# A kernel with a scheduler of its own: block counts, a load's place, a queue, row halves and stream shares are changed

## The chip, the cores and the metric

The kernel runs on one core of a Trainium2 chip. The metric is device time of one launch in microseconds (us), the median of several runs. TensorE is called PE here, VectorE DVE, ScalarE ACT, GpSimd POOL and SyncE SP, as the profile does.

## The reference

The program computes a forward pass and its gradient for all inputs but one. Cut to what matters:

```
xn  = layernorm(A_q)                                  # 2048 tokens x 512
ks  = sum over t<4 of shifted(A_k, 3-t) * shift_k     # a causal filter of 4 taps
kv  = ks * A_v
y   = causal_conv(kv, ssm_k) + kv * ssm_D             # by FFT of length 4096
s   = xn * y
h   = sigmoid(xn @ w_gate) * (xn @ w_up)              # 512 -> 1376
out = A_q + s * silu(h @ w_down)                      # 1376 -> 512
# returned: out, and the gradients for A_q, A_k, A_v, shift_k, ssm_k, ssm_D, w_gate, w_up, w_down
```

All tensors are bf16.

## The kernel before

**Recording and ordering.** The kernel doesn't issue its instructions as Python meets them. A recorder (`Rec`) takes every call with what it reads and writes. `Rec.order` then lists them: it keeps a modelled clock for each engine, takes the operation that can start first (ties by the order of recording), chooses ACT or DVE for copies that either can make (`evac`), and assigns PSUM banks. `emit` issues the program in that order, so one line of the code carries nearly all instructions: L566 those of PE in groups (bursts), L568 all others.

**Blocks in that model.** The model counts PE's instructions, two for each matmul (a weight load and the matmul), in blocks of `IBLK` = 256. `fetch` (L394) lets PE wait where a block ends sooner than a given time after the block before it. That time is 5.0 us for operations recorded before the mark `rec.late`, and one of the two values of `IFETCH` after it, the larger when the modelled hardware DMA queue is occupied. The count starts from `iblk` (L392). Where a short-tile burst would wait, a dense one may be taken ahead of it.

**Streams.** What is recorded when is set by `run_streams`: generators yield the amount of PE work that they have recorded, and the one with the lowest position goes on. The position runs from the first to the second of two shares (the last two numbers of each tuple), in step with the work done. A stream with a later start share, or a larger end share, is recorded later against the others.

**Stages.** In the first stage, `strG` computes layernorm, gate and up (eight pairs of token tiles), `strK` transforms the convolution kernel, and `strV` filters k, transforms kv, multiplies, and transforms back. Then `stepB` does the gate's backward pass. The last stage runs three streams: `dW` (weight gradients, dense matmuls 512, 352 and 320 wide from transposed loads), `frontC` (forward transform of the convolution's incoming gradient), and `backC`, inside `endC` (products with the stored spectra in DRAM, inverse transforms). `backC` handles four channel groups; after groups 1 and 3 it calls `taps` (L1416) for two groups each.

**`taps`** multiplies the convolution's gradient by v into `dks`, whose last three of nineteen rows hold rows of the neighbouring partitions, copied by two DMAs from `dks` itself. There is one `dks` buffer, so one group's taps wait for the last reader of the group before. `taps` then computes the gradient for shift_k on PE (groups of 128x32 matmuls) and the gradient for k as four multiply-and-add steps over sixteen rows of 128 channels, each a DVE operation of 2048 elements, and stores it to `o2C` in two halves after the second group of a pair.

**The start.** `make_identity` and four small memsets stand on POOL ahead of two small loads: `skT` (filter taps) and `Dcol_b` (ssm_D, the skip weights). POOL adds the skip weights to the first column of the convolution kernel (`KT`). DVE then copies `KT` into another order, and PE transposes it.

Of the kernel before, what the change touches and what calls it, by code (L numbers as in the profile page):

```python
# [10 lines left out]
ALU = mybir.AluOpType  # L11
# [6 lines left out]
P = 128  # L18
# [6 lines left out]
NJ = 16  # L25
# [138 lines left out]
class Rec:  # L164
# [3 lines left out]

    NEAR = 300
    BUBBLE = 0.12  # L170
    IBLK, IFETCH = 256, (4.2, 6.0)
    late = 1 << 30
    hold = None
    ENGS = ("tensor", "vector", "scalar", "gpsimd", "sync")
# [183 lines left out]
    def order(self):  # L358
# [30 lines left out]
        pipe = {"gpsimd": 0.0, "hw": 0.0, "act": 0.0}  # L389
        table = "sin"  # L390
        pemode = "full"
        iblk = [0, 0.0, self.IFETCH[0]]  # L392

        def fetch(op, t, occ, commit):  # L394
            n = 2 * (len(op.alts[0][2]) if op.alts[0][1] == "burst" else 1)
            k, b, gap = iblk
            wait = 0.0
            if k + n >= self.IBLK:
                wait = max(0.0, b + gap - (t + occ * (self.IBLK - k) / n))
                b = t + wait + occ * (self.IBLK - k) / n  # L400
                k -= self.IBLK
                gap = 5.0 if op.n < self.late else self.IFETCH[pipe["hw"] > b + 3.0]
            if commit:
                iblk[:] = [k + n, b, gap]
            return wait
# [166 lines left out]
def run_streams(streams, until=None):  # L572

    live = [list(st) + [0.0] * (5 - len(st)) for st in streams]
    while live:
        if until is not None and until():
            break
        for st in sorted(live, key=lambda s: s[2] + (s[3] - s[2]) * s[4] / s[1]):
            try:
                c = next(st[0])  # L580
            except StopIteration:
                live.remove(st)
                break
            if c:
                st[4] += c
                break
        else:
            raise RuntimeError("all streams blocked")
    return live


def make_identity(nc, ident):
    nc.gpsimd.memset(ident, 0.0)
    nc.gpsimd.affine_select(out=ident, in_=ident, compare_op=ALU.not_equal, fill=1.0,
                            base=0, pattern=[[-1, ident.shape[1]]], channel_multiplier=1)
# [64 lines left out]
def kernel_impl(ctx, tc, A_q, A_k, A_v, A_shift_k, A_ssm_k, A_ssm_D, B_x, B_w_gate, B_w_up, B_w_down,  # L660
# [25 lines left out]
    def dma2o(eng, dst, src):  # L686
        for r in range(2):
            eng.dma_start(dst[r], src[64 * r:64 * r + 64])
# [243 lines left out]
    def ld_w(eng, f0, f1):  # L932
        for w, src in ((wg, B_w_gate), (wu, B_w_up)):
            eng.dma_start(w[:, :, f0:f1], src[:, f0:f1].rearrange("(db p) f -> p db f", p=P))
    make_identity(nc, ident)
    nc.gpsimd.memset(kT[:, 0:16], 0.0)
    nc.gpsimd.memset(wg[:, :, F:FP], 0.0)
# [5 lines left out]
    for eng, r in ((nc.sync, 0), (nc.scalar, 1)):  # L943
        eng.dma_start(T[0]["xq"][64 * r:64 * r + 64], qC[r, :, 0:2, :])
    ld_w(nc.scalar, 0, 512)
    nc.gpsimd.dma_start(skT, A_shift_k.rearrange("(cg p) t -> p cg t", p=P))
    nc.gpsimd.dma_start(Dcol_b, A_ssm_D.rearrange("(cg p) -> p cg", p=P))
    ld_KT(0)
    ld_w(nc.sync, 512, 1024)
    ld_w(nc.sync, 1024, F)  # L950
# [34 lines left out]
    def strG():  # L985
        for q in range(8):
            if q == 0:
                n0 = len(rec.ops)
                f_ln(1)
                rec.ops[n0].deps.add(ln0 + 7)  # L990
                f_Tpe(1)
            if q + 2 < 8:
                f_ln(q + 2)
            if q + 3 < 8:
                f_x(q + 3)
            z = z_pre(q - 1) if q - 1 in ZA else iter(())
            for n, c in enumerate(f_gen(q)):
                yield c
                if n in (1, 3):
                    yield from islice(z, 1)  # L1000
            if q + 2 < 8:
                f_T(q + 2)
            if q == 1:
                nc.sync.dma_start(wd[:, 0:NFB - 1, :], B_w_down[0:128 * (NFB - 1), :].rearrange("(fb p) d -> p fb d", p=P))
                nc.sync.dma_start(wd[0:96, NFB - 1, :], B_w_down[128 * (NFB - 1):F, :])
# [104 lines left out]
            if cg % 2 == 1:  # L1110
                yield from inv1(B, y2A[:, :, c0 - GW:c1])

    run_streams([(strG(), 8 * 22528 + len(ZA) * 11264, -0.06, 1.07), (strK(), 4 * 8192, -0.14, 0.73), (strV(), 4 * 27648, -0.06, 0.97)])
    for r in (KT_r, KC_r, zt_r, kTp_r, kT_r, dg4_r, vg_r, acc_r, V_r, U_r, KS_r, XS_r, P1_r, B_r):
        r.free()

# [299 lines left out]
    def taps(cg):  # L1416
        c0, c1 = cg * GW, (cg + 1) * GW
        dkv = y2A[:, :, c0:c1]
        while "v" not in stC:
            yield 0  # L1420
        vg = stC["v"][:, :, c0:c1]
        dks = dks_r.next()
        nc.vector.tensor_tensor(dks[:, 0:NJ, :], dkv, vg, ALU.mult)
        nc.vector.memset(dks[96:P, NJ:NJ + 3, :], 0.0)
        nc.gpsimd.dma_start(dks[0:64, NJ:NJ + 3, :], dks[64:128, 0:3, :])
        nc.gpsimd.dma_start(dks[64:127, NJ:NJ + 3, :], dks[1:64, 0:3, :])
        nc.vector.tensor_tensor(dkv, dkv, stC["ksh"], ALU.mult)
        if cg + 1 < NG:
            ld_ksh(cg + 1)
        if cg % 2 == 1:  # L1430
            for j in range(0, NJ, 8):
                dma2o(nc.sync, o3C[:, :, j:j + 8, c0 - GW:c1], y2A[:, j:j + 8, c0 - GW:c1])
        yield 512
        pa = nc.ps("m1", [4, 32], f32)
        calls = []
        for j in range(NJ):
            for x in range(4):
                s = slice(32 * x, 32 * x + 32)
                calls.append(("matmul", (pa[s], dks[:, j, s], kh[:, j:j + 4, c0 + 32 * x:c0 + 32 * x + 32]), dict(start=(j == 0), stop=(j == NJ - 1))))
        nc.burst("128x32", 64 * 0.0157, calls)  # L1440
        dm = dm_r.next()
        nc.vector.tensor_tensor(dm, pa[:], I32[:, None, :].to_broadcast([P, 4, 32]), ALU.mult)
        nc.vector.tensor_reduce(res[:, cg, :], dm, AX.X, ALU.add)
        yield 2048
        dk = vg
        for lag in range(4):
            src = dks[:, lag:lag + NJ, :]
            skl = skb[:, lag:lag + 1, c0:c1].to_broadcast([P, NJ, GW])
            if lag == 0:
                nc.vector.tensor_tensor(dk, src, skl, ALU.mult)  # L1450
            else:
                term = dKT_r.next().rearrange("p (j c) -> p j c", c=GW)
                nc.vector.tensor_tensor(term, src, skl, ALU.mult)
                nc.vector.tensor_tensor(dk, dk, term, ALU.add)
            yield 512
        if cg % 2 == 1:
            for j in range(0, NJ, 8):
                dma2o(nc.sync, o2C[:, :, j:j + 8, c0 - GW:c1], stC["v"][:, j:j + 8, c0 - GW:c1])

    def endC():  # L1460
        yield from backC()
# [52 lines left out]
        ld_KK(m)  # L1514
    YS_r = Ring(ar, [2, 1024], n=2)
    V_r, U_r = Ring(ar, [64, 32, 2]), Ring(ar, [32, 32, 2], n=2)
    live = run_streams(live + [(dW(), 35 * 8192, 0.99, 1.42), (frontC(), 8 * 4096, 0.98, 1.42)], until=lambda: "B" in flags)
    pair(7)
    for r in [wgT_r, wuT_r, go_r, L0_r, L1_r, dxa_r, dxn_r, u1_r]:
        r.free()  # L1520
# [10 lines left out]
    ld_KK(2)  # L1531
    rec.late = len(rec.ops)
    dw, fr = live
    live = run_streams([(dw[0], dw[1] - dw[4], 0.0, 1.0), (fr[0], fr[1], 0.03, 0.7, fr[4]),
                        (gated(endC(), "back"), 4 * 20480, -0.05, 0.65)], until=lambda: "back" in flags)
    run_streams(live)
    rec.emit()

# [59 lines left out]
```

## Time and profile before

| | |
|---|---|
| median of 3 runs | 505.82 us |
| lowest and highest run | 499.06 and 506.52 us |
| the profiled execution | 505.26 us |
| its span, first to last instruction | 503.5 us |
| mean granted clock of PE | 0.986 |
| busy share of PE, DVE, ACT, POOL | 92%, 79%, 54%, 4% |
| moved by DMA | 112.74 MB, mean 224 GB/s |

The busy time of PE counts overlapping matmuls once, with modelled ends. In a row of the timeline, the start and the length come first, then engine, line, operation, output and input with shapes, and the count; what stands in brackets is the engine's idle time just before the row and what released it. "Issue" means that the engine waited for nothing that the profile shows. The chip has one PE clock for the core; "granted clock" 0.50 in a window means that it ran at half speed there.

### The profile page before, as it was taken

Reading aid. Unit: us, or ns where it says so; the run is one execution under the profiler, and the core shown is the slowest. Engines: PE = TensorE matmul, PEld = TensorE weight load, DVE = VectorE, ACT = ScalarE, POOL = GpSimd, SP = SyncE. Lnnn points to the kernel's source line nnn. Section 1 sums busy time; section 2 is a strip of 40 time slices with the busy share of each in tenths; the row PEclk is TensorE's granted clock in tenths of the full one; section 3 lists DMA queues with packets and bytes.
Section 4 is the critical chain, followed back from the end, with each engine's and each line's share of the span. In section 5 each row is a group of like instructions: output and inputs, shape, how many; then the busy total and the mean of one; then the engine's idle time right before and its main releaser. Section 6 shows DMA issues by size and latency. Waiting matters only on the chain.

```text
span 503.5 us, 13650 instructions
## 1 busy us (share of the span) xinstructions
PE 464.2 (92%) x5862; PEld 304.1 (60%) x5895; DVE 396.4 (79%) x663; ACT 272.7 (54%) x341; POOL 20.9 (4%) x40
## 2 busy tenths in 40 slices
PE   4999999999999989999999999999898879988984
PEld 3776767686758555566556646445455456666652
DVE  8689999668775699879998998569778479984691
ACT  6567788767665674355266247147466554444211
POOL 4000300000000000000000000100000000000000
PEclk9999999999999989999999999999999889999998
DMA  8999999936599899988978869996899895999954
GB/s 257 213 235 289 244 320 239 301 138 195 196 240 253 224 192 221 292 220 274 269 199 244 197 172 230 227 256 212 197 269 222 215 257 138 247 235 193 196 130 110
DMA packets 180980, 112.74 MB, mean 224 GB/s; under 512 B 101621, under 2 KB 166073, under 8 KB 180920
## 3 DMA queue, kind: packets, MB, share of 16 engines
q1 hardware_dynamic: 179432, 110.29, 88.3%
q10 hardware_dynamic: 1136, 1.18, 0.8%
q8 instruction: 46, 0.75, 0.7%
q0 software_dynamic: 352, 0.40, 0.4%
q14 instruction: 14, 0.11, 0.1%
HBM read 39.23 MB, written 47.62 MB: 172 GB/s over the span
## 4 chain that ended last, share of the span: by engine, by line
PE 61%; issue 13%; DMA 3%; DVE 3%; ACT 2%; POOL 0%; ACTq 0%; POOLq 0%
PE psum L566 61%; DMA slab<-slab 3%; DVE slab L568 3%; ACT slab L568 2%; PE psum L568 0%; POOL slab L568 0%; ACTq L568 0%; POOLq L568 0%
## 5 line engine op out<-in xcount | busy, mean ns | idle before, releaser
L566 PE MATMUL psum<-slab 128*128 128x256 bf16 (+10 forms) x5853 | 462.8, 266 | 31.9 <-issue 10.9
L566 PEld LDWEIGHTS <-slab 128*128 128x128 bf16 (+5 forms) x5886 | 303.4, 102 | 190.4 <-issue 51.4
L568 ACT CAST slab<-psum 128x1024 bf16<-128x1024 f32 (+4 forms) x260 | 214.0, 874 | 170.9 <-PE psum L566 146.7
L568 DVE TENSOR_TENSOR slab<-slab 128x1024 bf16<-128x1024 bf16 (+4 forms) x344 | 242.7, 758 | 24.3 <-ACT slab L568 11.6
L568 DVE CAST slab<-psum 128x1024 bf16<-128x1024 f32 (+2 forms) x34 | 39.5, 1170 | 37.4 <-PE psum L566 20.3
L568 ACT ACTIVATE slab<-psum 128x1024 bf16<-128x1024 f32 (+2 forms) x44 | 37.3, 853 | 33.9 <-PE psum L566 32.7
L568 DVE TENSOR_TENSOR slab<-psum,slab 128x1024 bf16<-128x1024 f32 (+2 forms) x28 | 28.2, 1008 | 13.2 <-PE psum L566 10.4
L568 DVE STREAM_TRANSPOSE slab<-slab 128x512 f32<-128x512 f32 x48 | 31.1, 685 | 3.0 <-ACT slab L568 2.8
L568 ACT ACTIVATE slab<-slab 128x512 bf16<-128x512 bf16 (+3 forms) x25 | 21.8, 889 | 16.5 <-DVE slab L568 16.4
L568 DVE SCALAR_TENSOR_TENSOR slab<-slab 128x512 bf16<-128x512 bf16 (+1 forms) x48 | 24.7, 530 | 3.8 <-ACT slab L568 3.4
L568 DVE TENSOR_SCALAR slab<-slab 128x1 f32<-128x1 f32 (+8 forms) x58 | 13.5, 266 | 2.1 <-POOL slab L568 1.6
L568 POOL TENSOR_TENSOR slab<-slab 128x2 f32<-128x2 f32 (+1 forms) x12 | 9.8, 821 | 79.6 <-DVE slab L568 69.9
L568 POOL MEMSET slab<- 128x128 bf16 (+3 forms) x7 | 3.1, 445 | 214.5 <-PE psum L566 177.8
L568 DVE BATCH_NORM_STATS2 slab<-slab 128x6 f32<-128x512 bf16 x16 | 10.4, 679 | 1.3 <-DMA slab<-in_A_q_dram 1.3
L568 POOL DMA_DIRECT2D slab<-slab x8 | 4.3, 535 | 158.1 <-ACT slab L568 85.2
L568 DVE COPY slab<-slab 128x1216 bf16<-128x1216 bf16 (+2 forms) x17 | 7.2, 446 | 4.2 <-ACT slab L568 4.2
L568 DVE SCALAR_TENSOR_TENSOR slab<-psum,slab 128x512 bf16<-128x512 f32 x10 | 6.7, 686 | 4.5 <-PE psum L566 4.5
L568 ACT ACT_TABLE_LOAD x2 | 2.6, 1283 | 2.5 <-issue 2.5
L568 DVE MEMSET slab<- 32x192 uint32 (+3 forms) x8 | 1.3, 165 | 1.9 <-PEq L1582 0.8
L568 DVE BATCH_NORM_AGGREGATE slab<-slab 128x2 f32<-128x6 f32 x16 | 2.4, 170 | 0.0
L568 PE MATMUL psum<-slab 128*4 128x128 bf16 (+1 forms) x9 | 1.8, 326 | 0.0
L568 POOL DMA_DIRECT2D slab<-in_A_shift_k_dram x2 | 1.5, 769 | 3.0 <-DMA sF_d<-slab 3.0
(15 smaller groups left out, 9.6 us busy)
## 6 DMA issues: line engine op xcount, KB each, us to landing
KK_d<-slab SPq DMA_DIRECT2D x16, 512.0 KB, 4.8
slab<-KK_d SPq DMA_DIRECT2D x16, 512.0 KB, 5.5
out_dram<-slab SPq DMA_DIRECT2D x58, 128.0 KB, 2.8
hS_d<-slab SPq DMA_DIRECT2D x8, 704.0 KB, 6.6
dgS_d<-slab SPq DMA_DIRECT2D x8, 704.0 KB, 4.8
duS_d<-slab SPq DMA_DIRECT2D x8, 704.0 KB, 6.0
sF_d<-slab SPq DMA_DIRECT2D x6, 704.0 KB, 5.7
slab<-sF_d SPq DMA_DIRECT2D x6, 704.0 KB, 6.8
```

Source lines behind the costliest of these rows:

```text
L566: getattr(self.nc.tensor, m)(*[place(v) for v in aa], **{x: place(v) for x, v in kk.items()})
L568: getattr(getattr(self.nc, eng), meth)(*[place(v) for v in a], **{x: place(v) for x, v in k.items()})
```

## The change

Five things change. In the model, `iblk` starts at 96 instead of 0 and without a first wait, the wait of 5.0 us before `rec.late` becomes 0, and the larger value of `IFETCH` becomes 6.5. At the start, the loads of `Dcol_b` and `skT` are recorded ahead of the identity and the memsets. In `taps`, the two row copies are issued by ACT instead of POOL. For the last channel group the four steps run over rows 0 to 7 and then rows 8 to 15, each half with its own store. And the shares of all streams but `stepB` and the remaining `dW` are new.

```diff
-    IBLK, IFETCH = 256, (4.2, 6.0)
+    IBLK, IFETCH = 256, (4.2, 6.5)
...
-        iblk = [0, 0.0, self.IFETCH[0]]
+        iblk = [96, 0.0, 0.0]
...
-                gap = 5.0 if op.n < self.late else self.IFETCH[pipe["hw"] > b + 3.0]
+                gap = 0.0 if op.n < self.late else self.IFETCH[pipe["hw"] > b + 3.0]
...
+    nc.gpsimd.dma_start(Dcol_b, A_ssm_D.rearrange("(cg p) -> p cg", p=P))
+    nc.gpsimd.dma_start(skT, A_shift_k.rearrange("(cg p) t -> p cg t", p=P))
     make_identity(nc, ident)
...
-    nc.gpsimd.dma_start(skT, A_shift_k.rearrange("(cg p) t -> p cg t", p=P))
-    nc.gpsimd.dma_start(Dcol_b, A_ssm_D.rearrange("(cg p) -> p cg", p=P))
...
-    run_streams([(strG(), 8 * 22528 + len(ZA) * 11264, -0.06, 1.07), (strK(), 4 * 8192, -0.14, 0.73), (strV(), 4 * 27648, -0.06, 0.97)])
+    run_streams([(strG(), 8 * 22528 + len(ZA) * 11264, -0.04, 1.02), (strK(), 4 * 8192, -0.07, 0.81), (strV(), 4 * 27648, 0.06, 0.94)])
...
-        nc.gpsimd.dma_start(dks[0:64, NJ:NJ + 3, :], dks[64:128, 0:3, :])
-        nc.gpsimd.dma_start(dks[64:127, NJ:NJ + 3, :], dks[1:64, 0:3, :])
+        nc.scalar.dma_start(dks[0:64, NJ:NJ + 3, :], dks[64:128, 0:3, :])
+        nc.scalar.dma_start(dks[64:127, NJ:NJ + 3, :], dks[1:64, 0:3, :])
...
-        for lag in range(4):
-            src = dks[:, lag:lag + NJ, :]
...
+        step = NJ if cg + 1 < NG else NJ // 2
+        for j0 in range(0, NJ, step):
+            js = slice(j0, j0 + step)
+            for lag in range(4):
+                src = dks[:, lag + j0:lag + j0 + step, :]
...
+            if cg % 2 == 1:
+                for j in range(j0, j0 + step, 8):
+                    dma2o(nc.sync, o2C[:, :, j:j + 8, c0 - GW:c1], stC["v"][:, j:j + 8, c0 - GW:c1])
...
-    live = run_streams(live + [(dW(), 35 * 8192, 0.99, 1.42), (frontC(), 8 * 4096, 0.98, 1.42)], until=lambda: "B" in flags)
+    live = run_streams(live + [(dW(), 35 * 8192, 0.89, 1.91), (frontC(), 8 * 4096, 0.87, 1.62)], until=lambda: "B" in flags)
...
-    live = run_streams([(dw[0], dw[1] - dw[4], 0.0, 1.0), (fr[0], fr[1], 0.03, 0.7, fr[4]),
-                        (gated(endC(), "back"), 4 * 20480, -0.05, 0.65)], until=lambda: "back" in flags)
+    live = run_streams([(dw[0], dw[1] - dw[4], 0.0, 1.0), (fr[0], fr[1], -0.21, 0.48, fr[4]),
+                        (gated(endC(), "back"), 4 * 20480, -0.15, 0.67)], until=lambda: "back" in flags)
```

More of the change, by code (lines that the diff above doesn't have):

```diff
@@ L1445, in taps @@
         dk = vg
-        for lag in range(4):
-            src = dks[:, lag:lag + NJ, :]
[L1448 to L1458, printed above, removed]
+        step = NJ if cg + 1 < NG else NJ // 2
[3 more added lines that the diff above has]
+                src = dks[:, lag + j0:lag + j0 + step, :]
+                skl = skb[:, lag:lag + 1, c0:c1].to_broadcast([P, step, GW])
+                if lag == 0:
+                    nc.vector.tensor_tensor(dk[:, js], src, skl, ALU.mult)
+                else:
+                    term = dKT_r.next().rearrange("p (j c) -> p j c", c=GW)
+                    nc.vector.tensor_tensor(term[:, js], src, skl, ALU.mult)
+                    nc.vector.tensor_tensor(dk[:, js], dk[:, js], term[:, js], ALU.add)
+                yield 32 * step
+            if cg % 2 == 1:
+                for j in range(j0, j0 + step, 8):
+                    dma2o(nc.sync, o2C[:, :, j:j + 8, c0 - GW:c1], stC["v"][:, j:j + 8, c0 - GW:c1])
     def endC():
```

## The prediction

> **What bounds the kernel now.** I read the view by windows first, cut where the work changes: the first stage to 180 us, the gate's backward to 335 us, the last stage to 500 us.
>
> ```profile
> 0.00:180.00 180.00, 165.94 (x2567) 122.47 (x2576) 143.43 (x242) 122.93 (x136) 15.29 (x31) 1.00 0.93 238
> ...
> 335.00:500.00 165.00, 146.25 (x2340) 93.96 (x2347) 122.83 (x158) 77.88 (x104) 4.27 (x8) 0.98 0.89 207
> ```
>
> The columns are the window, its length, then busy time and count for PE, weight loads, DVE, ACT and POOL, then granted clock, DMA share and GB/s. PE is the busiest engine in both rows, DVE is next with 80% and 74%. PE is not busy for 14.1 us of the first stage and 18.8 us of the last, so a better order can win at most these, what the clock costs, and what lies behind the last matmul.
>
> Next I looked at the longest waits of PE in the last stage, in the timeline.
>
> ```profile
> 393.59 2.83 PE L566 MATMUL psum<-slab 64*64 64x64 bf16 x31 [2.40 <-issue]
> ...
> 410.92 36.57 PE L566 MATMUL psum<-slab 128*32 128x128 bf16 x512 [2.76 <-issue]
> ```
>
> Both say "issue": no operand was late. They stand where a block of 128 pairs of weight load and matmul ends, counted from pair 92 of the program. Windows laid between two such places show it: each holds about 128 weight loads (second count).
>
> ```profile
> 354.42:360.87 6.45, 5.25 (x139) 2.94 (x134) 3.75 (x5) 3.29 (x4) 0.00 (x0) 1.00 1.14 228
> 372.60:378.18 5.58, 4.33 (x133) 3.26 (x132) 3.30 (x5) 4.30 (x6) 0.00 (x0) 1.00 1.01 305
> ...
> 386.84:393.58 6.74, 4.34 (x128) 3.22 (x128) 4.32 (x8) 1.92 (x3) 0.00 (x0) 0.99 1.06 276
> 403.14:410.93 7.79, 5.03 (x137) 3.74 (x131) 5.40 (x7) 5.67 (x8) 1.10 (x2) 0.98 1.24 228
> 442.59:448.14 5.55, 5.06 (x142) 3.82 (x134) 3.77 (x7) 2.94 (x5) 0.00 (x0) 1.00 1.11 252
> 457.12:459.97 2.85, 2.22 (x132) 2.08 (x132) 0.00 (x0) 0.63 (x1) 0.00 (x0) 1.00 1.33 148
> ```
>
> These six are the blocks of the last stage with the least work; they took 34.96 us together. PE waits there for its own instructions: block ends come no closer than 2.85 us and on average 5.83 us. In the first stage a block ended without such a wait after 3.88 us.
>
> ```profile
> 165.54:169.42 3.88, 3.88 (x145) 3.26 (x136) 2.90 (x4) 2.51 (x4) 0.00 (x0) 1.00 0.52 116
> ```
>
> The two long waits cost more than themselves. The next windows pair the 3.4 us that hold each with the 3.4 us behind it.
>
> ```profile
> 390.00:393.40 3.40, 1.18 (x76) 1.07 (x68) 1.16 (x2) 0.00 (x0) 0.00 (x0) 1.00 1.01 249
> 393.50:396.90 3.40, 3.31 (x34) 1.79 (x35) 0.75 (x2) 2.58 (x3) 0.00 (x0) 0.50 0.94 228
> 407.10:410.50 3.40, 1.06 (x61) 0.79 (x55) 1.47 (x2) 1.93 (x2) 0.15 (x1) 1.00 1.32 173
> 410.60:414.00 3.40, 3.08 (x20) 1.60 (x20) 2.54 (x5) 0.00 (x0) 0.00 (x0) 0.51 1.08 379
> ```
>
> After a stretch in which PE was busy 1.1 of 3.4 us, it runs the next 3.4 us at half clock. That is a loss of 1.7 us each.
>
> **The change, part by part.** The sum is made against the profiled execution, 505.3 us with a span of 503.5 us. It lies 0.1% under the median of the runs, 505.82 us.
>
> *Load first.* Both small GpSimd loads go ahead of the identity and four memsets.
>
> ```profile
> 0.85 0.47 POOL L568 IOTA slab<- 128x16 int32 x4 [0.40 <-POOLq L1582]
> ...
> 4.42 0.91 POOL L568 DMA_DIRECT2D slab<-in_A_ssm_D_dram  x1
> ...
> 10.89 0.21 POOL L568 TENSOR_TENSOR slab<-slab 128x1 bf16<-128x1 bf16 x1 [2.46 <-DMA slab<-in_A_ssm_D_dram]
> ...
> 11.22 0.68 DVE L568 COPY slab<-slab 128x2048 bf16<-128x2048 bf16 x1
> ...
> 11.96 16.52 PE L566 MATMUL psum<-slab 128*128 128x128 bf16 x160 [1.84 <-DVE slab L568]
> ```
>
> The skip column arrives at 10.89, the copy of the convolution kernel waits for it, and PE idles 1.84 us for the copy. Issued right behind the index tables (0.85 + 0.47), the load starts some 3 us sooner, and in the new order DVE copies ahead of the row normalisation. PE then does the sixteen transposes in its gap. The gain is 0 to 1.84 us; I take 1.0, because normalisation, and with it the first gate matmuls, moves back by the copy's 0.68. The identity is ready later by both loads, about 1.8 us. That is hidden, since PE's first matmul waits for ACT until 5.08 anyway:
>
> ```profile
> 5.07 1.63 PEld L566 LDWEIGHTS <-slab 128*32 128x32 bf16 x64 [5.07 <-ACT slab L568]
> ```
>
> Without that cover the delay would cost up to 1.8 us.
>
> *Block counts, new shares.* The order now places block ends at pairs 80, 208 and so on (the trace: 92, 220) instead of 128, 256. It no longer keeps block ends 5 us apart ahead of the last stage. I list both programs' PE instructions in their new and old order, cut them at pair 92 + 128n, and price each matmul by busy time over count.
>
> ```profile
> L566 PE MATMUL psum<-slab 128*128 128x512 bf16 x661 | 153.6, 379 | 2.7 <-issue 1.4
> L566 PE MATMUL psum<-slab 128*128 128x256 bf16 x1056 | 129.4, 277 | 4.0 <-ACT slab L568 3.2 <-DVE slab L568 0.7
> L566 PE MATMUL psum<-slab 128*128 128x352 bf16 x384 | 63.5, 321 | 0.0
> L566 PE MATMUL psum<-slab 64*128 64x128 bf16 x896 | 35.0, 218 | 4.9 <-issue 2.9 <-DVE slab L568 2.0
> ...
> L566 PE MATMUL psum<-slab 128*128 128x320 bf16 x128 | 18.2, 299 | 0.0
> L566 PE MATMUL psum<-slab 64*32 64x512 bf16 x384 | 17.3, 396 | 1.6 <-ACT slab L568 1.0 <-DVE slab L568 0.6
> L566 PE MATMUL psum<-slab 64*64 64x128 bf16 x512 | 9.4, 218 | 2.9 <-issue 1.5 <-DVE slab L568 1.4
> L566 PE MATMUL psum<-slab 64*64 64x64 bf16 x512 | 9.3, 195 | 2.9 <-issue 2.4 <-ACT slab L568 0.5
> L566 PE MATMUL psum<-slab 128*32 128x128 bf16 x384 | 8.5, 253 | 9.9 <-ACT slab L568 5.4 <-issue 2.8 <-DVE slab L568 1.8
> L566 PE MATMUL psum<-slab 32*128 32x64 bf16 x512 | 5.5, 191 | 0.0
> ```
>
> That gives 0.232, 0.123, 0.165, 0.039, 0.142, 0.045, 0.018, 0.018, 0.022 and 0.011 us. The block that ends at pair 5468, for one, was 128 matmuls of the 0.018 kind, 2.3 us; now it holds 124 of them and four of 0.165, 2.9 us. The six shortest blocks of the last stage held 5.56, 4.66, 4.45, 5.80, 5.33 and 2.30 us of work, 28.1 together, against 34.96 taken: 6.9 us of waiting. In the new order there are again six, of 4.91, 4.56, 5.32, 5.20, 2.89 and 4.36 us, 27.2 together. At the same mean distance they wait 7.8 us, 0.9 more. But by that mean no wait but one (5.83 - 2.89) comes near 2.4 us, and the block of that one had its successor ready after 2.85 us before; so I take both half-clock stretches as gone, -3.4. The term is -2.6. Its ends are -10.3 (6.9 and 3.4 both vanish) and +12.6 (six blocks at the longest distance, 7.79).
>
> In the first stage the shortest block held 4.2 us before. Now four hold 3.12, 5.26, 4.68 and 5.11 us. At 3.88 us one waits, 0.8 us; at 5.83 they cost 2.7 + 0.6 + 1.2 + 0.7 = 5.2 us. I take 0.8, the distance seen in that stage; the ends are 0 and +5.2.
>
> The Trainium skill ("Runtime: NRT & Kernel Launch", section on instruction fetch mechanics) says that the sequencer fetches the next 16 KiB block while it runs the current one, and that crossing a boundary is mostly hidden. By that rule both block terms would be nothing and the sum 502.3; the waits of 2.40 and 2.76 us above speak against it for short blocks.
>
> *Shifted rows on ScalarE's queue; row halves.*
>
> ```profile
> 465.82 1.07 POOL L568 DMA_DIRECT2D slab<-slab  x2 [38.69 <-DVE slab L568]
> ...
> 467.42 9.77 PEld L566 LDWEIGHTS <-slab 128*32 128x32 bf16 x124 [0.29 <-issue]
> ...
> 473.31 8.66 DVE L568 TENSOR_TENSOR slab<-slab 128x2048 bf16<-128x2048 bf16 x7 [4.14 <-DMA slab<-slab]
> ...
> 482.02 3.57 PE L566 MATMUL psum<-slab 128*32 128x128 bf16 x80 [1.82 <-DVE slab L568]
> ...
> 485.52 7.52 DVE L568 TENSOR_TENSOR slab<-slab 128x2048 bf16<-128x2048 bf16 x6
> ...
> 486.05 10.06 PE L566 MATMUL psum<-slab 128*128 128x352 bf16 x72
> ```
>
> From 467.42, where the third tap group's matmuls start, DVE needs 25.6 us to its end at 493.04, of which 4.14 is the wait for shifted rows that were issued at 465.82. The rows still wait for the same product, so I let 1.0 of the 4.14 remain, an estimate; the ends are 0 and all. On ACT the new issues wait for that product too, and casts stand behind them. Dependent PE groups go to four other banks in turn, each 16 matmuls of 0.165, so some 10 us of PE work lies between a late cast and PE; I cost it at nothing, and at the issues' 1.1 us a pair if that cover is gone. The halves turn seven 2048-wide operations of the last group (7.52 / 6 = 1.25 each) into fourteen 1024-wide ones:
>
> ```profile
> L568 DVE TENSOR_TENSOR slab<-slab 128x1024 bf16<-128x1024 bf16 x206 | 131.8, 684 | 8.1 <-ACT slab L568 7.2
> ```
>
> 131.8 / 206 = 0.64, fourteen times is 8.96 against 8.75: 0.2 more. DVE's chain becomes 25.6 - 3.1 + 0.2 = 22.7 us. Behind it only half the rows are left to store.
>
> ```profile
> 494.85 4.60 SPq L568 DMA_DIRECT2D out_dram<-slab  x5
> ```
>
> Five stores are issued over 4.60 us, and the span ends 8.65 us after the first. With two stores the issuing is 1.84, and 5.9 us remain. Against that, 32 more matmuls of 0.165 now stand ahead of the third tap group (100 of the 352-wide followed, now 68), so it starts 5.3 us later, at 472.7. The end is 472.7 + 22.7 + 0.1 + 5.9 = 501.4, which is 2.1 less than 503.5. If the shift is no faster it is +1.0. If only PE counts, 21.7 of its work is left at 472.7, and behind it come a cast, one issue (4.60 / 5) and the 4.05 us between the last issue's end and the span's:
>
> ```profile
> 496.15 0.42 ACT L568 CAST slab<-psum 128x320 bf16<-128x320 f32 x1 [1.75 <-PE psum L566]
> ```
>
> That makes 472.7 + 21.7 + 5.4 = 499.8, -3.7. I take -2.0.
>
> The Trainium skill ("Trainium Kernel Development and Optimization", Key Constraints) says that DMAs from SP, ACT and POOL share 16 DMA engines and that another queue saves only issue time. By it the 3.1 us would stay, and the sum would be 503.5, the last of the rivals; no run yet shows this copy on ACT's queue.
>
> The sum: 505.3 - 1.0 - 2.6 + 0.8 - 2.0 = 500.5 us.
>
> **The rivals.** *The late waits go altogether*: the six blocks wait for operands anyway, fetches are done by then, and PE sets the end. 505.3 - 1.0 - 10.3 + 0.8 - 3.7 = 491.1. For it: twelve pairs of error are at most 0.5 us in a block of short matmuls. Against it: the new order has as many short blocks as the old.
>
> *The count changes nothing*: the long waits and the half-clock stretches stay, now at other blocks. 505.3 - 1.0 + 0.9 + 0.8 - 2.0 = 504.0. For it: six against six.
>
> *Slower: first-stage blocks wait as the late ones do.* The place is the four short blocks before 180 us, the price 5.2 us at a distance of 5.83, and the late stretches stay: 505.3 - 1.0 + 0.9 + 5.2 - 2.0 = 508.4. With what is left on the other side (-2.1), it decides from a distance of 4.9 us, where 1.8 + 0.2 are lost. For it: the order no longer spaces these blocks, and DMA is as busy there (0.93) as late (0.89). Against it: 3.88 us sufficed once, and PE often waits there for ACT and DVE, which lengthens a block by itself.
>
> *The rule that fetches are hidden*: both block terms nothing and the rest as summed, 505.3 - 1.0 - 2.0 = 502.3. The waits on "issue" at 393.59 and 410.92 speak against it.
>
> *The shift is no faster*: 505.3 - 1.0 - 2.6 + 0.8 + 1.0 = 503.5. For it: the issues took 1.07 us, and the landing all the rest from 465.82 to 473.31. Against it: the other queue issues without GpSimd.
>
> **How the numbers follow.** I give the forecast 0.41, the late waits gone 0.22, nothing changed 0.12, slower 0.16, the hidden fetch 0.04 and the shift no faster 0.05. The likeliest gives 500.5 us, by itself 496 to 505. The whole reorder has parts that no row prices, so the range reaches a little beyond the outer cases: 490 to 512. Two per cent, about what a measurement of this kernel can tell from no change, is 495.7 and 515.9. Faster is the first rival's 0.22; slower by that much is a third of the slower case, in which late fetches lengthen as well, 0.06. The rest, 0.72, is within.
>
> **What would show it.** Right: PE's first 128-wide transposes after the tables start near 9 us; the shifted-row wait of DVE before the third group falls to about 1 us; two stores stand behind DVE's last operation; no stretch of half clock lies between 390 and 415 us. Wrong: waits on "issue" over 1 us before 180 us, waits of 2 us and more still in the last stage, or a wait of PE behind casts that stand behind ACT's new copies.

## The result and the profile after

The changed kernel's median is 496.43 us (493.37 to 501.38, 20 runs) against 502.54 us for the kernel before on the same chip (497.07 to 506.61, 20 runs). The ratio is 0.9906, 95% interval 0.988 to 0.9931: nearly 1% faster. All ratios here leave out slow runs, those over 1.5% above the fastest of their kernel, while the medians hold all runs, so the quotient of two medians (0.988 here) can lie lower, by up to 0.007. The profiled execution of the changed kernel took 501.08 us, 4.65 us above its median, with a span of 499.3 us; that of the kernel before took 505.26 us, 2.72 above its median of 20 runs. Differences between these two profiles are therefore not exact.

First the view by windows, of the kernel before and of the changed one. Both are cut at the same instructions of PE: weight loads 2652 and 3420, where the gate's backward pass begins and ends, and the last weight load. Columns as in the prediction.

```profile
0.00:191.79 191.79, 175.68 (x2643) 130.41 (x2652) 154.42 (x265) 130.75 (x149) 15.29 (x31) 0.99 0.92 235
191.79:314.36 122.57, 121.83 (x757) 70.41 (x768) 109.35 (x224) 58.70 (x82) 0.00 (x0) 1.00 0.89 233
314.36:495.66 181.30, 166.24 (x2464) 103.19 (x2474) 132.63 (x177) 82.80 (x110) 5.64 (x9) 0.98 0.91 210
495.66:503.50 7.84, 0.45 (x4) 0.10 (x1) 0.00 (x0) 0.42 (x1) 0.00 (x0) 0.73 0.58 144
```

```profile
0.00:189.48 189.48, 174.16 (x2645) 130.20 (x2653) 156.26 (x264) 127.64 (x146) 11.93 (x31) 0.98 0.90 235
189.48:312.05 122.57, 121.73 (x757) 70.44 (x769) 110.94 (x226) 59.08 (x82) 0.00 (x0) 1.00 0.92 237
312.05:492.65 180.60, 169.41 (x2461) 104.16 (x2475) 132.21 (x184) 82.68 (x110) 1.37 (x1) 0.96 0.90 213
492.65:499.30 6.65, 0.38 (x3) 0.05 (x1) 0.53 (x1) 0.77 (x2) 0.00 (x0) 0.73 0.53 131
```

Of the 4.2 us between the spans, 2.3 lie in the first stage, none in the backward pass (122.57 both times), 0.7 in the last stage and 1.2 behind the last weight load. In the last stage PE is idle 3.9 us less (15.06 to 11.19) but busy 3.2 us longer, at a clock of 0.96 instead of 0.98.

The start, in the timeline of the changed kernel. POOL now waits last for a part of the convolution kernel, no longer for ssm_D, and PE's first 128-wide transposes start at 9.48 instead of 11.96.

```profile
1.47 0.94 POOL L568 DMA_DIRECT2D slab<-in_A_ssm_D_dram  x1 [0.15 <-issue]
...
8.50 0.96 POOL L568 TENSOR_TENSOR slab<-slab 128x1 bf16<-128x1 bf16 x2 [3.27 <-DMA slab<-in_A_ssm_k_dram]
8.73 0.69 DVE L568 COPY slab<-slab 128x2048 bf16<-128x2048 bf16 x1 [0.67 <-POOL slab L568]
9.48 3.74 PE L566 MATMUL psum<-slab 128*128 128x128 bf16 x35 [0.34 <-DVE slab L568]
```

The block that I had feared in the first stage, the one with 3.12 us of work, ran through 129 matmuls in 3.75 us; PE shows no wait for "issue" over 0.16 us in that stage's timeline.

```profile
94.80:98.55 3.75, 3.02 (x129) 2.27 (x130) 3.62 (x6) 3.40 (x4) 0.00 (x0) 1.00 0.64 170
```

PE's waits for "issue" at block ends of the last stage are three, where the kernel before had seven of 0.49 to 2.76 us. Together they are 4.96 us, against 9.48. Waits of 0.16 us are left out in both, and one of 0.33 us that stands between two block ends.

```profile
376.97 1.62 PE L566 MATMUL psum<-slab 64*32 64x512 bf16 x37 [2.40 <-issue]
443.43 6.08 PE L566 MATMUL psum<-slab 64*128 64x128 bf16 x70 [1.54 <-issue]
459.06 23.82 PE L566 MATMUL psum<-slab 64*64 64x128 bf16 x300 [1.02 <-issue]
```

At two of them PE then runs 6.8 us each at half clock, twice as long as before. Windows of the changed kernel:

```profile
376.50:379.90 3.40, 2.59 (x40) 1.38 (x41) 3.40 (x7) 2.00 (x2) 0.00 (x0) 0.50 1.14 278
379.90:383.30 3.40, 3.40 (x46) 1.44 (x44) 2.47 (x5) 0.44 (x1) 0.00 (x0) 0.53 0.14 46
458.20:461.60 3.40, 2.54 (x58) 1.95 (x59) 0.80 (x1) 1.12 (x2) 0.00 (x0) 0.50 0.78 208
461.60:465.00 3.40, 3.40 (x41) 1.82 (x40) 0.43 (x1) 1.08 (x2) 0.00 (x0) 0.50 0.57 121
```

The tail, in the timeline of the changed kernel:

```profile
468.56 1.48 ACTq L568 DMA_DIRECT2D slab<-slab  x2
471.01 11.54 PEld L566 LDWEIGHTS <-slab 128*32 128x32 bf16 x136 [0.29 <-DVE slab L568]
472.67 8.65 DVE L568 TENSOR_TENSOR slab<-slab 128x2048 bf16<-128x2048 bf16 x7
482.81 0.22 PE L568 MATMUL psum<-slab 128*4 128x128 bf16 x1
482.96 8.89 PE L566 MATMUL psum<-slab 128*128 128x320 bf16 x120
491.03 2.15 DVE L568 TENSOR_TENSOR slab<-slab 128x1024 bf16<-128x1024 bf16 x3
```

The third tap group starts at 471.01; DVE doesn't wait for the shifted rows at 472.67 (4.14 us before); its last operation ends at 493.18. PE finds matmuls to run between the tap groups and never waits for DVE there.

### The profile page after: what moved, and what is told of

Same layout as the page of the kernel before. It is cut to its first block, busy times and chain, and to the rows that moved or that the text cites. A ratio compares the mean times of both kernels' runs of the same rounds, so it can differ in the third digit from the quotient of the medians.

```text
span 499.3 us, 13661 instructions
## 1 busy us (share of the span) xinstructions
PE 465.7 (93%) x5859; PEld 304.8 (61%) x5895; DVE 399.9 (80%) x672; ACT 270.2 (54%) x339; POOL 13.3 (3%) x32
## 4 chain that ended last, share of the span: by engine, by line
PE 74%; DVE 13%; DMA 4%; issue 3%; ACT 3%; POOL 0%; ACTq 0%; SPq 0%; DVEq 0%; POOLq 0%
PE psum L566 74%; DVE slab L568 13%; ACT slab L568 3%; DMA slab<-in_A_ssm_k_dram 3%; DMA slab<-slab 1%; PE psum L568 0%; POOL slab L568 0%; ACTq L568 0%; SPq L568 0%; DVEq L568 0%; POOLq L568 0%
## 5 line engine op out<-in xcount | busy, mean ns | idle before, releaser
L568 ACT CAST slab<-psum 128x1024 bf16<-128x1024 f32 (+3 forms) x258 | 212.2, 871 | 173.6 <-PE psum L566 149.1
L568 DVE CAST slab<-psum 128x1024 bf16<-128x1024 f32 (+1 forms) x36 | 42.2, 1177 | 24.7 <-ACT slab L568 14.6
L568 POOL TENSOR_TENSOR slab<-slab 128x2 f32<-128x2 f32 (+1 forms) x12 | 6.7, 566 | 81.0 <-DVE slab L568 68.4
L568 DVE DVE_READ_ACCUMULATOR slab<-slab 128x1 f32 x16 | 1.3, 82 | 0.0
```

The lines of the kernel that those rows point to most:

```text
L568: getattr(getattr(self.nc, eng), meth)(*[place(v) for v in a], **{x: place(v) for x, v in k.items()})
```

## The experiments

"Ratio" is to the kernel before on the same chip, with the 95% interval. The versions stand on three chips, and the whole change was not run beside them, so rows from different chips compare only roughly. The first four do one part of the change alone, the next four leave one part out.

| version | ratio | medians, this and before (us) |
|---|---|---|
| block count alone | 1.0088 (1.0059 to 1.0117) | 503.05, 499.69 |
| new shares alone | 1.0131 (1.0084 to 1.0178) | 505.26, 499.69 |
| load first alone | 1.0073 (1.0038 to 1.0108) | 502.70, 499.69 |
| ACT's queue and halves alone | 0.9979 (0.994 to 1.0018) | 499.26, 499.69 |
| all but the new shares | 1.0133 (1.0083 to 1.0183) | 506.72, 503.08 |
| all but the block count | 0.997 (0.993 to 1.001) | 498.07, 503.08 |
| all but the load first | 0.9995 (0.995 to 1.004) | 500.31, 503.08 |
| all but the halves | 0.9965 (0.9927 to 1.0003) | 499.04, 503.08 |
| the whole change | 0.9906 (0.988 to 0.9931) | 496.43, 502.54 |

**Block count alone.**

```diff
-    IBLK, IFETCH = 256, (4.2, 6.0)
+    IBLK, IFETCH = 256, (4.2, 6.5)
-        iblk = [0, 0.0, self.IFETCH[0]]
+        iblk = [96, 0.0, 0.0]
-                gap = 5.0 if op.n < self.late else ...
+                gap = 0.0 if op.n < self.late else ...
```

> The kernel before with the new block count alone (start at 96, no 5 us spacing, 6.5 for the larger wait); shares, loads, queue and halves as before. By my block arithmetic four blocks of the last stage fall under 5.6 us of work (4.61, 5.50, 4.57, 4.65) where six did; at a mean distance of 5.83 us they wait 4.0 us instead of 6.9, so 2.9 us less: ratio 0.994. Rival, the shares make the gain: the count alone gives 1.000 within 0.002.

Slower by 0.9%, where I expected a gain. PE did gain: in its profile the last stage to the last weight load is 7.4 us shorter than before, without a half-clock stretch. But the end did not follow. Windows of that version, the last stage and what lies behind its last weight load:

```profile
311.40:485.35 173.95, 164.01 (x2466) 101.87 (x2475) 128.00 (x174) 82.67 (x110) 5.65 (x9) 1.00 0.90 217
485.35:499.28 13.93, 0.43 (x4) 0.09 (x1) 5.58 (x5) 0.43 (x1) 0.00 (x0) 0.65 0.45 114
```

DVE still has 5.58 us of taps to do after PE is finished, and 13.93 us pass behind PE instead of 7.84: with the old shares of the streams and the old tail, 6.1 of the 7.4 us that PE gains are given back there. That explains a small gain, not a loss. The profiled execution, 501.06 us, lies 2.0 under the version's median and 4.2 under the profiled execution of the kernel before. What makes the version slower in the medians, no run shows.

**New shares alone.**

```diff
-... (strK(), 4 * 8192, -0.14, 0.73), (strV(), 4 * 27648, -0.06, 0.97)])
+... (strK(), 4 * 8192, -0.07, 0.81), (strV(), 4 * 27648, 0.06, 0.94)])
...
-... (gated(endC(), "back"), 4 * 20480, -0.05, 0.65)]
+... (gated(endC(), "back"), 4 * 20480, -0.15, 0.67)]
```

> The kernel before with the new shares alone. By the block arithmetic the last stage has six short blocks (2.95, 5.25, 4.96, 3.73, 4.07, 5.24), which wait 8.8 us instead of 6.9: ratio 1.004. Rival, the shares make the gain: about 0.993.

Slower by 1.3%, more than I expected. In its profile the first stage takes 193.87 us, PE idle 21.0 of them, against 191.79 and 16.1: the shares by themselves cost in the stage for which they place the streams anew. The short blocks that I blamed did not do it: PE's waits for "issue" in the last stage are 0.43 and 0.73 us, where I expected 8.8 in all, and that stage is 3.9 us shorter (177.40).

**Load first alone.**

```diff
+    nc.gpsimd.dma_start(Dcol_b, ...)
+    nc.gpsimd.dma_start(skT, ...)
     make_identity(nc, ident)
...
-    nc.gpsimd.dma_start(skT, ...)
-    nc.gpsimd.dma_start(Dcol_b, ...)
```

> The kernel before with both small loads first on GpSimd's queue, and nothing else; the order answers to it in the whole program. My term: 1.0 us at the start, and three short late blocks (4.61, 4.57, 4.07), which wait 2.7 us less: ratio 0.993. Rival, the load is hidden and a reorder by itself gives nothing: 1.000 within 0.002. The second block of 128 pairs ends at 21.3 us before; with the load first it ends at 19 to 20 us.

Slower by 0.7%, where I expected a gain. PE's first 128-wide transposes did start early, at 9.85 us, and DVE's copy at 9.10. But the order made from there on is another one, and its profile has PE's early end and the late tail again. That the order is what costs is argued, not shown: this span, too, is shorter than the 503.5 us before.

```profile
314.92:487.19 172.27, 164.42 (x2466) 102.16 (x2475) 126.97 (x175) 82.71 (x109) 5.64 (x9) 1.00 0.92 219
487.19:500.65 13.46, 0.43 (x4) 0.09 (x1) 4.99 (x5) 0.43 (x1) 0.00 (x0) 0.59 0.44 112
```

**ACT's queue and halves alone.**

```diff
-        nc.gpsimd.dma_start(dks[0:64, NJ:NJ + 3, :], ...)
+        nc.scalar.dma_start(dks[0:64, NJ:NJ + 3, :], ...)
...
-        for lag in range(4):
+        for j0 in range(0, NJ, step):
+            for lag in range(4):
```

> The kernel before with the shifted rows on ScalarE's queue and the row halves, and nothing else; the order of PE's matmuls stays as before up to the last groups. My steps: DVE's wait of 4.14 us before the third tap group falls to 1 us or less, DVE ends 3 us sooner, only two stores follow it, and PE's end, then the later of the two, leaves a gain of about 2 us: ratio 0.996. Rival, the transfers land no sooner from another queue and PE's dense matmuls end last anyway: 1.000 within 0.002, with the wait still near 4 us.

0.9979, with 1 and my 0.996 both inside the interval. In its profile 4.31 us lie behind the last weight load, against 7.84 before. But DVE's wait for the shifted rows did not fall to 1 us:

```profile
0.00:189.02 189.02, 172.62 (x2644) 128.66 (x2653) 152.65 (x262) 130.35 (x148) 15.93 (x31) 0.99 0.91 237
...
468.02 8.66 DVE L568 TENSOR_TENSOR slab<-slab 128x2048 bf16<-128x2048 bf16 x7 [2.99 <-DMA slab<-slab]
```

The window shows something else. PE's weight loads have the same shapes in the same order as in the kernel before until well into the last stage, so this is a second look at the old first stage: 189.02 us, where the other profile had 191.79. A difference of 2.8 us in that stage between two profiles need not come from the order.

**All but the new shares.** The diff of "new shares alone", reversed in the changed kernel.

> The changed kernel with the shares of before. First theory, balance: what the shares set is whether PE's dense matmuls of the last stage and the chain through DVE and the taps end together. The count alone and the load alone ended PE at 485 and 487 us and DVE at 491 and 492; with all but the shares it should be the same, PE's last weight load 4 us or more ahead of DVE's last operation, and the ratio to before near 1.003 (the tail's 2 us taken off 1.007). Rival, the block count makes the gain and the shares only go with it: 0.995.

This loses the whole gain and is 1.3% slower than the kernel before. My theory had PE done well ahead of DVE. PE was done after it (499.9 and 497.2 us), yet for the reason that I had in mind: PE waited for DVE. Timeline of that version:

```profile
490.66 0.27 PE L568 MATMUL psum<-slab 128*4 128x128 bf16 x1 [2.48 <-DVE slab L568]
...
495.12 0.37 PE L568 MATMUL psum<-slab 128*4 128x128 bf16 x1 [3.46 <-DVE slab L568]
```

The groups by line and shape, from the start of the third tap group to the end, tell why. The 352-wide matmuls there, in the kernel before:

```profile
L566 PE MATMUL psum<-slab 128*128 128x352 bf16 x101 | 15.9, 313 | 0.0
```

In the changed kernel:

```profile
L566 PE MATMUL psum<-slab 128*128 128x352 bf16 x69 | 10.6, 313 | 0.0
```

In the version without the new shares, whose third group starts at 473.46:

```profile
L566 PE MATMUL psum<-slab 128*128 128x352 bf16 x41 | 6.5, 313 | 0.0
```

The small sums over DVE's reductions (128*4) stand in PE's queue ahead of the last sixteen dense matmuls. Besides 64 of the 320-wide in each version, 69 of the 352-wide are left for the changed kernel's tail, and the sums wait for nothing; with 41, PE runs dry and stands 6.7 us at them (2.48, 3.46, and two short waits), and the sixteen start at 496.15. So the new shares leave the tail more dense work in this order. This is a part of the loss: of the 5.5 us between the spans of the two profiles (504.83 and 499.3), 3.1 lie behind the third group's start (31.37 against 28.29) and 2.6 in the first stage (192.09 against 189.48).

**All but the block count.** The diff of "block count alone", reversed.

> The changed kernel with the block count of before (from 0, 5 us apart, 6.0). Block arithmetic: four blocks of the last stage hold only 2.35, 2.73, 3.14 and 2.30 us of work, which wait 12.8 us at 5.83 us a block where the changed kernel's wait 7.8: 5 us slower than the changed kernel, ratio to before 1.000. Rival, block waits hide behind other waits and balance alone counts: 0.991 as with everything, if PE and DVE end within 3 us of each other.

0.997 against 0.9906: by the ratios the count is worth about 0.6% in the new order, by the medians less (0.990 and 0.988), and the intervals touch (0.993 and 0.9931), so this is not shown clear of noise. I had 1.000, from 12.8 us of block waits; the profile has three, 1.24, 0.94 and 2.23 us, together 4.41, less than the changed kernel's 4.96. So these profiles do not show the count's worth in the block waits.

**All but the load first.** The diff of "load first alone", reversed.

> The changed kernel with both small loads in their old place. My term is 1.0 us at the start and 2 us of block waits (4.07, 3.91, 4.69 us where 4.91, 4.56, 5.32 stood): ratio 0.997. Rival, the load is hidden behind the rest of the first stage: 0.991. The second block of pairs ends at 17.7 us with the load first; without it, near 20.

0.9995: without it the gain is gone, or most of it (the medians are still 2.8 us apart). That is more than the 2.5 us by which the transposes come sooner, so two things were mixed: the load, and the order that follows from it. A later run splits them.

**All but the halves.** The loop over `j0` undone.

> The changed kernel without the row halves: the order is the same up to the last tap group. By my steps four stores stand behind DVE's end instead of two, 2.8 us more of issuing, and DVE's chain is 0.2 us shorter: 2.5 us slower than the changed kernel, ratio to before 0.9955. Rival, PE's last cast and its store end the kernel anyway: 0.991.

0.9965, close to the 0.9955 expected; the halves are worth about 0.6% by that, with intervals that just overlap. Behind DVE's last operation 8.5 us pass (488.26 to 496.79) instead of the changed kernel's 6.1: 2.4 us more, where I had priced 2.5. Its order is that of the changed kernel up to the last tap group, so its profile is a second look at the same work. It came through the last stage in another way. First its timeline of PE, then that of the weight loads:

```profile
376.10 5.47 PE L566 MATMUL psum<-slab 64*32 64x512 bf16 x121 [1.15 <-issue]
```

```profile
466.08 11.54 PEld L566 LDWEIGHTS <-slab 128*32 128x32 bf16 x136 [0.29 <-DVE slab L568]
```

At the same block end PE waited 1.15 us instead of 2.40 and kept full clock behind it, and the third tap group started at 466.08 instead of 471.01. The same instructions in the same order thus differ by almost 5 us from one run to another.

**The queue by itself.** The changed kernel's order, with the row copies of the last stage put on POOL's queue as they are issued:

```diff
+                if eng == "scalar" and meth == "dma_start" and op.n >= self.late:
+                    eng = "gpsimd"
                 getattr(getattr(self.nc, eng), meth)(
```

> The changed kernel with every instruction in its order; only the eight shifted-row transfers of the last stage are issued from POOL's queue in place of ScalarE's. In the changed kernel VectorE doesn't wait before the third tap group, before the change it waited 4.14 us there. Theory (it is the queue): the wait is back at about 3 to 4 us, the third tap group starts near 474, and the ratio to the kernel before goes from 0.9906 to about 0.9965. Rival (the rows land as early from either queue, the wait went with the order): no wait over 1 us, ratio 0.991.

0.9882 (0.9847 to 0.9917; 496.06 and 503.75 us). The rival's number, not mine: the queue doesn't show in the time. In the timeline a part of the wait is back, though the rival had it under 1 us.

```profile
464.95 1.05 POOL L570 DMA_DIRECT2D slab<-slab  x2 [41.51 <-DVE slab L570]
...
470.55 8.66 DVE L570 TENSOR_TENSOR slab<-slab 128x2048 bf16<-128x2048 bf16 x7 [1.66 <-DMA slab<-slab]
```

From issue to use are 5.60 us (470.55 - 464.95), in the changed kernel 4.11 at most (472.67 - 468.56), before the change 7.49 (473.31 - 465.82). By these two profiles ACT's queue spares DVE 1.7 us of the 4.1 at the third group, and 1.0 of it is left at DVE's end (23.2 us from the third group's start instead of 22.2). How much of the wait is the queue is not settled by one profile of each. In the order before, with POOL's queue, the last version below waits 2.12 us instead of 4.14, and from issue to use it needs 5.47 us (471.59 - 466.12), no more than this version does:

```profile
471.59 8.66 DVE L571 TENSOR_TENSOR slab<-slab 128x2048 bf16<-128x2048 bf16 x7 [2.12 <-DMA slab<-slab]
```

With ACT's queue the old order waits 2.99. The issue itself takes longer on ACT, 1.48 us a pair against 1.05.

**The late load by itself.** The changed kernel's order on all engines, with only the two small loads issued behind the memsets on POOL again:

```diff
+        loads = [s for s in seq if eng_of(s) == "gpsimd" and s[0].dma][:2]
+        seq = [s for s in seq if all(s is not v for v in loads)]
+        at = next(i for i, s in enumerate(seq) if eng_of(s) == "gpsimd" and s[0].alts[s[1]][1] == "tensor_tensor")
+        seq[at:at] = loads[::-1]
```

> The changed kernel with every other engine's instructions in its order; only the two small loads stand on POOL's queue behind the memsets again. Theory (the landing counts by itself): VectorE's first table copy goes from 8.7 back to about 11.2 us and the first 128-wide transposes from 9.5 to about 12, the later stages shift by 1 to 2.5 us, ratio 0.994 to 0.996 in place of 0.9906. Rival (the load matters only by the order that it gave, which this kernel keeps): the first transposes are late, the first boundary of stages is not, ratio 0.991; then the loss of the version with the old start, 0.9995, is all order.

0.9936 (0.9897 to 0.9974; 498.81 us). The load counts by itself, as the first theory had it.

```profile
10.21 0.96 POOL L573 TENSOR_TENSOR slab<-slab 128x1 bf16<-128x1 bf16 x2 [4.89 <-DMA slab<-in_A_ssm_D_dram]
10.44 0.69 DVE L573 COPY slab<-slab 128x2048 bf16<-128x2048 bf16 x1 [2.38 <-POOL slab L573]
11.19 2.05 PE L571 MATMUL psum<-slab 128*128 128x128 bf16 x17 [2.04 <-DVE slab L573]
```

The copy is 1.71 us later than in the changed kernel, PE's wait for it 1.70 us longer (2.04 against 0.34), and weight load 2652 comes 2.1 us later, at 191.57; with the early load in the same order, two other profiles have it at 189.85 and 187.97. The medians on this chip are 2.75 us apart (498.81 and 496.06, the queue's version, whose order is that of the changed kernel; the means of twelve runs each are 2.6 apart, over three times the standard error of that difference). What the version with the old start lost beyond this, 0.9995 against 0.9936, may be the order; the intervals overlap.

**The count from 72.**

```diff
-        iblk = [96, 0.0, 0.0]
+        iblk = [72, 0.0, 0.0]
```

> The changed kernel with the planner's count starting at 72 in place of 96, so that its blocks end nearer to pair 92, where the trace shows them. Theory (the count is worth what it spares in block waits): the long waits of the last stage go from a sum of about 6 us to 4 or less, ratio 0.987 to 0.990. Rival (any count that starts this late does as well, the rest is the draw of the order): 0.991 within its interval, the waits of single blocks moved but not shorter in sum; a worse order could give 0.995 and more.

0.9857 (0.9804 to 0.9911; 495.38 us), a little better than either theory had it. It has the lowest median here and beats the kernel before; its interval overlaps with the changed kernel's, and the queue's version on the same chip is 0.7 us away, so it is not shown to beat that. The waits for "issue" moved but did not shrink as the theory said, 4.55 us in all against 4.96:

```profile
374.08 1.76 PE L566 MATMUL psum<-slab 128*128 128x512 bf16 x73 [1.60 <-issue]
...
438.82 6.08 PE L566 MATMUL psum<-slab 64*128 64x128 bf16 x70 [1.12 <-issue]
454.74 21.20 PE L566 MATMUL psum<-slab 128*128 128x352 bf16 x300 [1.83 <-issue]
```

**Block ends moved, order kept.** The kernel before, with 92 repeats of PE's first matmul ahead of all:

```diff
+                    if self.dup:
+                        a, self.dup = [a[0]] * self.dup + list(a), 0
                     for m, aa, kk in a:
```

> The kernel before with its order unchanged; 92 repeats of TensorE's first matmul are put at its start, so that the real ends of blocks, 92 pairs behind the planner's count before, stand where that count had them. [...] Theory (blocks that end where they were counted wait less, with no other change): the sum of block waits in the last stage falls from about 12 us by 2.7 to 6, ratio 0.990 to 0.997. Rival (the waits of blocks stand beside other waits and only trade places): waits fall, but the last stage is as long as before, ratio 1.000 to 1.003.

1.0122 (1.006 to 1.0185; 507.69 us), outside both ranges, which left little room for what the repeats cost in the first stage. Windows of this version to weight load 2744 and of its last stage, and PE's first rows:

```profile
0.00:194.49 194.49, 176.59 (x2735) 133.50 (x2744) 152.56 (x262) 130.30 (x148) 14.61 (x31) 1.00 0.91 230
...
317.06:494.09 177.03, 164.51 (x2464) 102.46 (x2474) 132.53 (x177) 82.54 (x110) 5.63 (x9) 0.99 0.93 216
```

```profile
5.07 9.50 PE L569 MATMUL psum<-slab 128*32 128x128 bf16 x223 [5.07 <-ACT slab L571]
18.04 7.21 PE L569 MATMUL psum<-slab 128*128 128x128 bf16 x89 [3.47 <-issue]
```

The repeats filled the first blocks with short matmuls, and PE waited 3.47 us for "issue" at the end of the second; the first stage became 2.7 us longer. The last stage is 4.3 us shorter in this profile (177.03 against 181.30), and its waits for "issue" are 2.60, 0.79 and 3.23 us, 6.62 in all against 9.48 (not the 12 that I had taken), which fits the theory; but this execution, 503.57 us, lies 4.1 under the version's median. Whether block ends in the right place pay without any other change stays open.

## Why the prediction was right, and where it wasn't

The ratio that I forecast, 500.5 / 505.3 = 0.9905, is the one measured, 0.9906. So close a hit is luck: the terms were less good than their sum. In us the forecast was 4.1 too high (500.5 against 496.43), most of it because it started from a profiled execution 2.7 us above the median of 20 runs; between the medians lie 6.1 us, where I had 4.8. From the two profiles, by the prediction's own cuts:

- *Load first*: predicted -1.0 (0 to -1.84). The first stage is 2.3 us shorter, which two profiles alone don't prove, as the second look at the old order shows (189.02). With the order held, the load by itself is worth 2.1 us in the profile of the late load and 2.75 in the medians. The mechanism was right (POOL's wait, DVE's copy, PE's transposes, which start at 9.48, as foreseen near 9); the term is mis-sized, because I took half of PE's gap of 1.84 as likely. With the load late, DVE's copy comes 1.71 us later and PE waits 1.70 us longer, and this came through whole to the end of the stage. Whether DVE carries it there, busy for 82% of the stage (156.26 of 189.48), or PE, busy for 92% (174.16), no run shows.
- *First-stage blocks*: predicted +0.8 (0 to +5.2). Nothing: the shortest block took 3.75 us without a wait. The rival that these blocks wait as the late ones do fell.
- *Late blocks*: predicted -2.6, from +0.9 of waits and -3.4 of clock (which make -2.5; the sum has a slip of 0.1). From the backward pass's end to the third tap group were 153.06 us before (467.42 - 314.36) and 158.96 after (471.01 - 312.05), less the 5.3 of the moved matmuls: +0.6. The two halves of the term were both wrong and nearly cancelled, in the other direction each: the waits fell by 4.5 us (9.48 to 4.96), and the half-clock stretches did not go; there are none between 390 and 415 us, as I wrote, but 6.8 us each at 376 and 458 (and two of 3.4 us in the first stage, at 45 and 69, where the kernel before has one, at 182). A wait of 2.40 us was named as a sign of being wrong, and it came. In other runs of the same order up to that place the same term is -4.7 (all but the halves: 466.08 - 312.42 - 5.3 against 153.06), -1.8 (the queue: 467.14 - 310.55) and -2.0 (the late load: 470.46 - 314.14): the four come to -2.0 in the mean, near my -2.6, for reasons other than mine, and less so against the second look at the old order, where this stretch, in almost the same order, took 151.71 us (463.30 - 311.59) instead of 153.06. The failing step is the use of one mean distance of block ends, 5.83 us: the waits at a block end are not set by its work alone, as the same block end with 2.40 and 1.15 us shows. The same arithmetic gave 4.0, 8.8 and 12.8 us of waits for the count alone, the shares alone and all but the count; their profiles show 1.82, 1.16 and 4.41. Nor do these waits go with the time: the count, the shares and the load alone wait least for "issue" in the last stage (1.82, 1.16 and 1.53 us) and are slower than the kernel before.
- *Tail*: predicted -2.0. The 32 dense matmuls moved ahead of the third tap group as counted (101 to 69 behind its start), +5.3; from that start to the end are 28.29 us instead of 36.08, -7.8: -2.5. Most of its numbers held: start at 472.7 foreseen and 471.0 found, DVE's chain 22.7 and 22.2, behind DVE 5.9 and 6.1. The 4.14 us of the wait went altogether rather than to 1.0, and four stores, not two, are issued from 493.02 on, in 2.26 us. I gave 3.1 us of the wait to ACT's queue; by the queue's version it is 1.7, and even that is uncertain, since the wait on POOL's queue alone was 4.14, 2.12 and 1.66 us in three profiles. The Trainium skill's rule that another queue saves only issue time ("Trainium Kernel Development and Optimization", Key Constraints) is nearer to the times, which do not tell the queues apart, than my step was; in one profile of each queue the rows come 1.5 us sooner from issue to use with ACT's.
- *What no step had*: the shares. The prediction treats them only by what they put into blocks and ahead of the third tap group. Alone they cost 1.3%, and without them the rest is 1.3% slower than before instead of 0.9% faster. The load is needed as well (0.9995 without it). By the sum of single parts (0.88 + 1.31 + 0.73 - 0.21) the change would have cost 2.7%. A sum of terms could come near only because I cut both finished orders, where the shares' effect on dense work (101 to 69) was already counted.

Together -2.3, 0, +0.6 and -2.5 make the 4.2 us between the spans. Of the rivals, "the count changes nothing" (504.0) would be a ratio of 0.997 and "the shift is no faster" (503.5) one of 0.996, both outside the interval; "late waits go altogether" and the hidden fetch fell with the 4.96 us of waits that are left.

## What to carry to other kernels

Where a planner orders the program, a part of a change has no price of its own: compare the finished orders, count what dense work is left to fill the tail, and test parts by holding the emitted order and altering one thing. A stage that ends on one engine's chain can give back what another engine gains ahead of it, as in the profiles of the block count and of the early load alone. A small load at the start can cost its whole delay (here the copy came 1.7 us later, and the medians are 2.75 us apart), not half of the gap that shows on PE. And one profile of each order is not enough for a difference of 2 us in one stage: take a second run of the same order first.

## What the runs showed of the hardware

Half clock outlasts the idle that brings it on. In the changed kernel PE was busy 2.59 of the 3.4 us from 376.50 at half clock, and the next 3.4 us ran at 0.53 although PE was busy throughout; before, a wait was followed by one stretch of 3.4 us, with PE busy 3.31 and 3.08 us in the two that the prediction shows. This holds in all profiles of this case: of 34 half-clock stretches before 470 us, 26 last 3.4 us, and PE is busy for 2.93 us or more in each (the least in the block count alone, at 11.5 us); the other eight last 6.8 us, and in their first 3.4 us PE is busy for 2.79 us or less (the most in the load first alone, at 63.0 us). Each of the 34 began behind 3.4 us in which PE was busy for about 2.5 us or less. Runs of one kernel differ by this: over 20 runs of the changed kernel time and mean granted clock go together with a correlation of -0.89, 1.32 us for each 0.0034 of clock, which is one such stretch in 500 us. And the wait at one and the same block end differed between runs of one order, 2.40, 2.67, 2.28 and 1.15 us, with what stood before it unchanged; what decides it no run here shows.
